# Chunk bounds and selection of a quad: 576 queries in one pass in place of 192 and 384, with new instruction lists

## The chip, the cores and the metric

One core of a Trainium2 chip runs the whole kernel; seven cores are idle. The metric is the device time of one execution in microseconds (us). Each number of runs is given with its median. Before the change three runs gave 272.13 us as median (272.02 to 273.0).

## What is computed

Two layers, one after the other, for 4 batches of 768 tokens.

The first is attention with 8 heads of 64 and a choice of key chunks. Keys are cut into 24 chunks of 32. For each query and chunk an upper bound of the score is formed from the smallest and the largest key value of each dimension:

```
k_min, k_max = min and max of k over the 32 keys of a chunk
ub  = sum over d of max(q * k_min, q * k_max)          # (query, chunk)
ub  = -1e9 where the chunk lies behind the query's own
top = the 6 chunks with the largest ub
attn = softmax of q.k/8 over the keys of these chunks, causal
x   = attn @ v
```

A query of the first 192 has at most six chunks in front of it, so for it nothing has to be chosen. The choice concerns the other 576 queries.

The second is a two-layer network on the 3072 rows of 512: `h = x @ w_in` (2048 wide), `g = h where h > 0, else exp(h) - 1`, `out = g @ w_out`.

## The kernel before, in words

**Tiling.** Two heads of a batch make a pair (16 pairs, numbered 0 to 15, four to a batch); two pairs make a quad (8 quads). The 768 queries of a pair are two halves of 384. Batch 0 (`SPLIT`) is loaded, turned and prepared half by half (`first_prep`, L637): TensorE (PE) turns K and Q by transposes (L689), ScalarE (ACT) copies them out of PSUM (L699, L721, L725), VectorE (DVE) reduces the chunks' minima and maxima (L708). Pairs of batches 1 to 3 are prepared whole (`pair_prep`): DVE transposes (L607, L625) and reduces (L611), GpSimd (POOL) casts to bf16 (L741).

**Chunk bounds and selection.** `quad_sel` (L744) handles a quad and a half: the first half has 192 queries that need a choice, the second 384. Its steps are:

- PE forms the bounds of the quad's four heads (L771, 16 matmuls in float32 of 64 rows by 32 columns, the even and odd blocks of queries on different columns of the array) into one of two double PSUM buffers, `S2`.
- DVE transposes them into `ubt` (L788), sets the query's own chunk and those behind it to a very low value (L793), takes the eight largest of each block of 32 queries (L800, 6 or 12 instructions), compares the bounds with the sixth (L805, into `selv`) and transposes the result back (L811, into `selt`).
- Four copies on POOL (L822) put the result into rows 64 to 87 of the pair's query operand (`rhs`, held by `qb`). The keys' operand holds -40000 in the matching row and chunk, so that the score matmul itself masks the keys.

**Attention.** `pair_attend` computes scores (L863, into the same two `S2` buffers), the exponential on ACT (L890), the product with V (L922), the normalisation on DVE (L935, L938), a transpose on PE (L947) and a copy on ACT (L950) into `xT`. In batch 0 the diagonal is masked by PE (L869), later by POOL (L909).

**The network.** `mlp` runs for each batch and half: 16 blocks of four up-matmuls (L972), exponential (L982) and two DVE steps each (L1011 and L1016, or L987 on ACT and L990), then 12 groups of four down-matmuls (L1032), copies (L1041) and stores (L1046). It starts when the transposed attention output of its half is complete; batch 0's network runs beside batch 1's attention, and so on.

**What sets the order.** Every step is a numbered operation of a planner (`Plan`, L156), numbered in the order of the `add` calls. `QUEUE` (L52) is a list of these numbers for each engine, written out by hand: each engine issues its operations in exactly that order. The planner's durations only decide how the engines' lists are interleaved in the program and which buffer of a class an operation takes (`caps`, L405: for instance two `S2`, two `ubt`). PE, ACT, DVE and POOL each run their list in order, and SP starts most loads and all stores; four early Q loads are started by ACT. `PAUSE`, `ALONE` and `late` describe to the planner when loads arrive.

Of the kernel before, what the change touches and what calls it, by code (L numbers as in the profile page):

```python
# [74 lines left out]
    ],  # L75
    "POOL": [
# [12 lines left out]
    ],  # L89
    "ACT": [  # L90
# [20 lines left out]
    ],  # L111
# [5 lines left out]
    ],  # L117
# [43 lines left out]
class Plan:  # L161
# [71 lines left out]
    SHARE = {128: 1.0, 256: 0.35, 512: 0.3, 768: 0.3, 1024: 0.3, 2048: 0.5}  # L233
    HEAVY = 0.088
    RAMP = 240.0
    PAUSE = ((15.8,16.6),(21.9,22.7),(29.8,30.8))
    LANDED = 0.75

    def served(self, rings, t, until):
# [154 lines left out]
def kernel(  # L394
# [349 lines left out]
    def quad_sel(g, hf):  # L744

        pairs = (2 * g, 2 * g + 1)
        if hf == 0:
            SELT[g], = new("selt")
# [366 lines left out]
```

## Time and profile before

| | |
|---|---|
| median of 3 runs | 272.13 us |
| the profiled execution | 271.44 us |
| its span | 269.6 us |
| PE busy | 260.3 us |
| DVE busy | 207.2 us |
| ACT busy | 200.6 us |
| POOL busy | 122.3 us |
| matmuls for the chunk bounds (L771), all 16 calls | 512 records |

The profiled execution lasts a little longer than the span that its trace covers. Busy times of one engine overlap at their ends, since the next instruction starts while the last one drains, so a busy engine is not always at its peak. In a row of the chain of waits or of a timeline stand the start, the length, the engine, the line and the operation; in a row by line stand the shapes, the count, the busy time in us, the mean of one in ns, and the idle time before. In the table by stage, each engine's busy time and number of instructions follow the stage's length; the last three columns are the granted clock, the share of DMA and GB/s.

### The profile page before, as it was taken

The numbers are of one execution on the slowest core, as the hardware profiler recorded it, in microseconds if no ns is written. First come the engines' busy times: TensorE is split into PE (matmuls) and PEld (weight loads), VectorE is DVE, ScalarE is ACT, GpSimd is POOL, SyncE is SP. The second block draws the span as 40 slices with busy tenths as digits, with TensorE's granted clock in tenths as the row PEclk, the third lists the DMA queues.
The fourth block names the chain that finished last, engine by engine and source line by source line (L and its number), as shares of the span: only waits on it lengthen the run. The fifth ranks groups of instructions, "written<-read, shape, count | busy, mean of one in ns | idle before, by whom it ended". The sixth has DMA issues, their size and how long they took to land.

```text
span 269.6 us, 7062 instructions
## 1 busy us (share of the span) xinstructions
PE 260.3 (97%) x2648; PEld 162.8 (60%) x2648; DVE 207.2 (77%) x562; ACT 200.6 (74%) x375; POOL 122.3 (45%) x233
## 2 busy tenths in 40 slices
PE   4998899999999999999999999999999999999995
PEld 3986566655566655655655566565666555654544
DVE  5789899899999999999898946686666785444440
ACT  4899899757996989998999386986888843234322
POOL 3697971175995798745871167434610000000000
PEclk9999999999999999999999999999999999999999
DMA  7998999989996998999621020000030100102103
GB/s 222 268 233 118 203 215 213 182 165 163 186 174 106 191 212 152 165 180 221 127 80 41 0 80 0 2 2 1 2 117 4 39 0 24 58 2 78 72 6 119
DMA packets 112626, 29.82 MB, mean 111 GB/s; under 512 B 101200, under 2 KB 109648, under 8 KB 112592
## 3 DMA queue, kind: packets, MB, share of 16 engines
q1 hardware_dynamic: 107280, 24.39, 46.0%
q0 software_dynamic: 4224, 4.19, 9.4%
q10 hardware_dynamic: 1088, 0.79, 0.9%
q8 instruction: 21, 0.34, 0.6%
q14 instruction: 13, 0.11, 0.1%
HBM read 27.26 MB, written 6.29 MB: 124 GB/s over the span
## 4 chain that ended last, share of the span: by engine, by line
PE 90%; ACT 5%; DVE 2%; DMA 1%; issue 1%; POOL 0%; ACTq 0%
PE psH L972 23%; PE psM L1032 23%; PE psS L863 13%; PE psO L922 8%; PE psS L972 8%; PE psMT L1032 8%; PE psS L771 3%; ACT lhs L699 2%; ACT pt L890 2%; PE psT L947 2%; DMA gT<-in_k_dram 1%; PE psMT L689 1%; PE psH L689 1%; PE psS L869 1%; ACT qa L725 0%
## 5 line engine op out<-in xcount | busy, mean ns | idle before, releaser
L890 ACT ACTIVATE pt<-psS 128x768 bf16<-128x768 f32 (+2 forms) x120 | 89.9, 777 | 7.7 <-PE psO L922 4.0
L972 PE MATMUL psH<-xT,w_in_sb 128*128 128x384 bf16 x384 | 75.0, 326 | 0.0
L1032 PE MATMUL psM<-w_out_sb,gT 128*128 128x512 bf16 x288 | 71.8, 379 | 0.0
L972 PEld LDWEIGHTS <-w_in_sb 128*128 128x128 bf16 x512 | 47.8, 97 | 33.0 <-issue 1.2
L1032 PEld LDWEIGHTS <-gT 128*128 128x128 bf16 x400 | 37.4, 97 | 33.6
L982 ACT ACTIVATE f<-psH 128x384 f32<-128x384 f32 x96 | 48.1, 505 | 10.8 <-PE psH L972 8.8
L863 PE MATMUL psS<-rhs,lhs 88*128 88x384 bf16 (+4 forms) x304 | 54.5, 283 | 0.7 <-ACT pt L890 0.5
L909 POOL TENSOR_SCALAR_AFFINE_SELECT pt<-pt 128x512 bf16<-128x512 bf16 (+1 forms) x48 | 24.6, 521 | 48.3 <-ACT pt L890 47.6
L1011 DVE SCALAR_TENSOR_TENSOR t<-f,psH 128x384 bf16<-128x384 f32 x56 | 30.2, 544 | 10.8 <-ACT f L982 10.0
L822 POOL COPY rhs<-selt 24x192 bf16<-24x192 bf16 (+1 forms) x64 | 27.2, 424 | 22.2 <-DVE selt L811 19.6
L863 PEld LDWEIGHTS <-lhs 88*128 88x128 bf16 x304 | 27.6, 97 | 14.6 <-ACT pt L890 1.5
L741 POOL CAST rhs<-f 64x768 bf16<-64x768 f32 (+1 forms) x40 | 28.2, 706 | 13.4 <-DVE f L625 6.5
L1016 DVE SCALAR_TENSOR_TENSOR gT<-psH,t 128x384 bf16<-128x384 f32 x56 | 30.5, 549 | 1.0
L922 PEld LDWEIGHTS <-pt 128*128 128x128 bf16 x672 | 27.2, 98 | 6.0 <-ACT pt L890 0.6
L922 PE MATMUL psO<-vext,pt 128*128 128x65 bf16 x672 | 29.7, 194 | 0.3 <-ACT pt L890 0.2
L741 POOL CAST lhs<-f 64x768 bf16<-64x768 f32 x24 | 19.7, 821 | 12.1 <-DVE f L607 11.1
L982 ACT ACTIVATE f<-psS 128x768 f32<-128x768 f32 x16 | 12.9, 811 | 16.5 <-PE psS L972 16.4
L990 DVE SCALAR_TENSOR_TENSOR gT<-f,psH 128x384 bf16<-128x384 f32 x40 | 21.6, 543 | 3.6 <-ACT psH L987 3.1
L972 PE MATMUL psS<-xT,w_in_sb 128*128 128x384 bf16 x128 | 22.9, 326 | 0.0
L1000 DVE TENSOR_SCALAR t<-f 128x768 bf16<-128x768 f32 x16 | 8.9, 558 | 17.5 <-ACT f L982 17.5
L1032 PE MATMUL psMT<-w_out_sb,gT 128*128 128x512 bf16 (+1 forms) x112 | 22.1, 349 | 0.0
L950 ACT ACTIVATE xT<-psT 128x384 bf16<-128x384 bf16 x32 | 15.4, 498 | 8.4 <-PE psT L947 8.3
(55 smaller groups left out, 299.3 us busy)
## 6 DMA issues: line engine op xcount, KB each, us to landing
out_dram<-osb SPq DMA_DIRECT2D x23, 256.0 KB, 2.3
f<-in_k_dram SPq DMA_DIRECT2D x48, 96.0 KB, 4.1
f<-in_q_dram SPq DMA_DIRECT2D x48, 96.0 KB, 3.5
f<-in_v_dram SPq DMA_DIRECT2D x24, 192.0 KB, 3.8
w_in_sb<-in_moe_w_in_dram POOLq DMA_DIRECT2D x4, 512.0 KB, 8.0
w_out_sb<-in_moe_w_out_dram POOLq DMA_DIRECT2D x4, 512.0 KB, 12.4
gT<-in_k_dram SPq DMA_DIRECT2D x8, 192.0 KB, 4.0
gT<-in_v_dram SPq DMA_DIRECT2D x12, 128.0 KB, 4.3
```

The source lines that it names most:

```text
L741: nc.gpsimd.tensor_copy(out=o, in_=i)
L822: eng.tensor_copy(out=dst.rearrange("c h (i two x) -> c h i two x", two=2, x=32)[:, :, :, odd, :], in_=tiles[st][r0:r0 + NCH, c0:c0 + n].r ...
L863: nc.tensor.matmul(p_s[:, hd, pc:pc + w], lhsT=tiles[pt_["kb"]][0:64 + NCH, hd, 128 * kb:128 * kb + 128], rhs=tiles[pt_["qb"]][0:64 + NCH, ...
L890: lambda bs=bs, pt=pt, wtot=wtot, lo=lo, at=at: nc.scalar.activation(out=tiles[pt][:, :, lo:lo + wtot], in_=tiles[bs[0]][:, :, at:at + wto ...
L909: nc.gpsimd.affine_select(out=a, in_=a, compare_op=AOT.is_ge, fill=0.0, base=0, pattern=pat, channel_multiplier=-1)
L922: nc.tensor.matmul(po[:, hd, qi, :], lhsT=tiles[pt][:, hd, off:off + 128], rhs=tiles[pt_["vx"]][:, 6 * hd + kb, :], start=(kb == 0), stop= ...
L972: nc.tensor.matmul(ph, lhsT=w_in_sb[:, kk, f0:f0 + 128], rhs=tiles[XT[4 * b + kk]][:, c0:c0 + HALF], start=(kk == 0), stop=(kk == NKK - 1))
L982: lambda e=e, view=view: nc.scalar.activation(out=halves(e)[:, 0:step], in_=view(), func=AF.Exp),
L990: lambda e=e, view=view, fc=fc, gt=gt: nc.vector.scalar_tensor_tensor(out=tiles[gt][:, fc:fc + step, :], in0=halves(e)[:, 0:step], scalar= ...
L1011: lambda e=e, t=t, view=view: nc.vector.scalar_tensor_tensor(out=tiles[t][:, 0:step], in0=halves(e)[:, 0:step], scalar=1.0, in1=view(), op ...
L1016: lambda t=t, view=view, fc=fc, gt=gt: nc.vector.scalar_tensor_tensor(out=tiles[gt][:, fc:fc + step, :], in0=view(), scalar=0.0, in1=tiles ...
L1032: nc.tensor.matmul(pm, lhsT=tiles[gt][:, fc, 128 * tt:128 * tt + 128], rhs=w_out_sb[:, fc, x0:x1], start=(fc == 0), stop=(fc == NFC - 1))
```

## The change

For batches 1 to 3, whose pairs are prepared whole, `quad_sel` is called once for a quad with `hf = None`: 576 queries in one pass. So one call of 16 matmuls of 288 columns stands for two calls of 96 and 192 columns, one transpose into `ubt` for two, 18 maxima for 6 and 12, one comparison for two, one transpose back for two, and four copies on POOL of 24 x 576 for eight. In batch 0 the two halves stay. That is nine operations fewer for each of six quads, 54 in all (6 on PE, 24 on DVE, 24 on POOL).

`ubt`, `thr` and `selv` grow to 18 blocks; `ubt` and `thr` have one buffer in place of two.

The lists of all engines are new. All numbers behind the first selection of batch 1 are shifted; apart from that the order itself differs, in batch 0 too: DVE writes the zero rows ahead of the diagonal's tile, POOL makes the diagonal second in place of third, SP loads K of pair 0's second half second, PE issues the bounds of batch 0's second quad (operation 122) two places earlier and turns K of pair 0's second half before the first scores. The planner's description of loads is changed (`ALONE`, `PAUSE`, no `late`); it emits no instruction.

```diff
 QUEUE = {
     "DVE": [
-        0, 6, 7, 9, 11, 12, 8, 10, 22, 23, 24, 38, 39, 40, 56, 57, 82, 83, 58, 72, 73, 172, 74, 173, 84, 85,
+        6, 0, 7, 8, 11, 9, 12, 10, 22, 23, 38, 39, 40, 24, 56, 57, 82, 58, 72, 73, 83, 172, 74, 84, 173, 85,
...
     "POOL": [
-        3, 5, 1, 4, 28, 29, 44, 45, 30, 62, 46, 63, 78, 64, 80, 79, 179, 178, 87, 86, 88, 89, 180, 194, 195,
+        3, 1, 5, 4, 28, 29, 30, 44, 62, 45, 46, 78, 79, 63, 64, 179, 194, 86, 87, 195, 80, 178, 129, 127, 130,
...
     "SP": [
-        13, 31, 47, 163, 65, 17, 51, 165, 183, 215, 181, 197, 167, 217, 199, 201, 511, 513, 528, 530, 545, 559,
...
+        13, 163, 31, 47, 17, 65, 165, 217, 183, 51, 181, 197, 201, 215, 199, 511, 167, 513, 528, 530, 545, 525,
...
     "PE": [
-        19, 25, 41, 35, 53, 59, 69, 90, 75, 81, 169, 106, 175, 131, 185, 191, 203, 122, 147, 93, 219, 209, 109,
...
+        19, 25, 35, 41, 59, 53, 69, 75, 169, 81, 106, 175, 90, 191, 185, 122, 203, 131, 93, 209, 219, 225, 147,
...
-            "ubt": 2, "thr": 2, "selv": 2, "selt": 2, "pt": 10, "t": 3, "gT": 3,
+            "ubt": 1, "thr": 1, "selv": 2, "selt": 2, "pt": 10, "t": 3, "gT": 3,
...
-        "selv": [const.tile([P, 12, 32], BF16, name=f"selv{i}") for i in range(caps["selv"])],
+        "selv": [const.tile([P, 18, 32], BF16, name=f"selv{i}") for i in range(caps["selv"])],
...
-        "kx": ([P, NCH], F32), "ubt": ([P, 12, 32], F32), "thr": ([P, 12, 8], F32),
+        "kx": ([P, NCH], F32), "ubt": ([P, 18, 32], F32), "thr": ([P, 18, 8], F32),
...
     def quad_sel(g, hf):
 
         pairs = (2 * g, 2 * g + 1)
+        whole = hf is None
+        hs = (0, 1) if whole else (hf,)
+        end = whole or hf == 1
+        hf = 0 if whole else hf
...
-            n = HALF - SEL0 if hf == 0 else HALF
+            n = S - SEL0 if whole else HALF - SEL0 if hf == 0 else HALF
...
             for u in pairs:
-                rd += [PAIR[u]["qt", hf], PAIR[u]["qa", hf], (PAIR[u]["km"], 0, hf), (PAIR[u]["km"], 1, hf)]
-                if hf or u in SPLIT:
-                    fr += [PAIR[u]["qt", hf], PAIR[u]["qa", hf]]
-                if hf:
+                rd += [PAIR[u]["qt", hf], PAIR[u]["qa", hf]] + [(PAIR[u]["km"], i, x) for i in range(2) for x in hs]
+                fr += [PAIR[u]["qt", hf], PAIR[u]["qa", hf]]
+                if end:
                     fr += [PAIR[u]["km"]]
...
-                        reads=[(st, hf)], writes=[(qb, hf, odd, "left")], free=[st] if hf and j and odd else [],
+                        reads=[(st, x) for x in hs], writes=[(qb, x, odd, "left") for x in hs],
+                        free=[st] if end and j and odd else [],
...
             for g in (2 * b, 2 * b + 1):
-                for hf in range(2):
-                    quad_sel(g, hf)
+                quad_sel(g, None)
                 for u in (2 * g, 2 * g + 1):
                     for hf in range(2):
                         pair_attend(u, hf)
```

More of the change, by code (lines that the diff above doesn't have):

```diff
@@ L230, in clocked @@
         return dur if warm else dur + dur
-    ALONE = {128: 0.0138, 256: 0.0194, 512: 0.036, 768: 0.038, 1024: 0.055, 2048: 0.085}
+    ALONE = {128: 0.0138, 256: 0.0188, 512: 0.036, 768: 0.0368, 1024: 0.055, 2048: 0.085}
     SHARE = {128: 1.0, 256: 0.35, 512: 0.3, 768: 0.3, 1024: 0.3, 2048: 0.5}
@@ L235 @@
     RAMP = 240.0
-    PAUSE = ((15.8,16.6),(21.9,22.7),(29.8,30.8))
+    PAUSE = ((0.0, 2.28), (17.2, 17.8), (21.6, 22.4), (30.5, 31.3))
     LANDED = 0.75
@@ L571, in weights, with fetch @@
         add("DMA", 0.0, -20.0, lambda: None, reads=[("asked", i)], writes=[name], lat=plan.LANDED)
-    def fetch(starts, packets, size, pr, f, writes, eng="SP", more=(), late=0.0, **kw):
+    def fetch(starts, packets, size, pr, f, writes, eng="SP", more=(), **kw):
         uid[0] += 1
@@ L577, in fetch @@
         add(eng, 0.533 * starts, pr, f, reads=more, writes=[w] + writes, lat=0.0,
-            move=(0 if eng == "SP" else 1, (1.08 if eng == "SP" else 1.3) + late, 0.533, starts, packets, size), **kw)
+            move=(0 if eng == "SP" else 1, 1.08 if eng == "SP" else 1.3, 0.533, starts, packets, size), **kw)
         add("DMA", 0.0, pr, lambda: None, reads=[w], writes=writes, lat=plan.LANDED)
@@ L674, in first_prep @@
         early = u - SPLIT[0] < EARLY[hf]
-        late = 0.35 if u == SPLIT[0] and hf == 0 else 0.0
-        fetch(1, 256, 768, pl, load(i0, kr), [(sg, i0)], late=late, alloc=[sg] if u == SPLIT[0] else [])
+        fetch(1, 256, 768, pl, load(i0, kr), [(sg, i0)], alloc=[sg] if u == SPLIT[0] else [])
         fetch(1, 256, 768, (pl + 0.1) - 300.0 * early, load(i0 + 1, qr, nc.scalar if early else nc.sync), [(sg, i0 + 1)],
-              eng="ACT" if early else "SP", late=late)
+              eng="ACT" if early else "SP")
         if u % 2 == 0:
@@ L776, in quad_sel @@
             for u in pairs:
-                rd += [PAIR[u]["qt", hf], PAIR[u]["qa", hf], (PAIR[u]["km"], 0, hf), (PAIR[u]["km"], 1, hf)]
-                if hf or u in SPLIT:
-                    fr += [PAIR[u]["qt", hf], PAIR[u]["qa", hf]]
-                if hf:
+                rd += [PAIR[u]["qt", hf], PAIR[u]["qa", hf]] + [(PAIR[u]["km"], i, x) for i in range(2) for x in hs]
+                fr += [PAIR[u]["qt", hf], PAIR[u]["qa", hf]]
+                if end:
                     fr += [PAIR[u]["km"]]
-            add("PE", 0.0025 * n + 0.073, pr, ub, reads=rd, writes=[bu[0]], alloc=bu, free=fr)
+            add("PE", 0.00167 * n + 0.27, pr, ub, reads=rd, writes=[bu[0]], alloc=bu, free=fr)
             ut, = new("ubt")
@@ L812, in t2 @@
                                     in_=tiles[sv].rearrange("p a b -> p (a b)")[:, 0:n])
-            add("DVE", dve(n), pr, t2, reads=[sv], writes=[(st, hf)], alloc=[] if hf else [st], free=[sv])
+            add("DVE", dve(n), pr, t2, reads=[sv], writes=[(st, x) for x in hs], alloc=[] if hf else [st], free=[sv])
             for j, u in enumerate(pairs):
```

165 rows, old and new, of the table QUEUE are left out of this document.

## The prediction

> **What bounds the kernel now.** I read the page first: its head, the busy times, the forty slices.
>
> ```profile
> span 269.6 us, 7062 instructions
> PE 260.3 (97%) x2648; PEld 162.8 (60%) x2648; DVE 207.2 (77%) x562; ACT 200.6 (74%) x375; POOL 122.3 (45%) x233
> PE   4998899999999999999999999999999999999995
> PEclk9999999999999999999999999999999999999999
> ```
>
> TensorE is busy 97% of the span at full granted clock. To see whether it is dense where the change acts, I cut the span into stages (us, then busy time of PE, PEld, DVE, ACT, POOL):
>
> ```profile
> 10.00:20.00 10.00, 9.67 (x163) 8.77 (x160) 8.27 (x36) 9.82 (x26) 7.94 (x18) 1.00 1.14 250
> 20.00:32.50 12.50, 10.80 (x189) 7.88 (x187) 11.67 (x51) 11.56 (x24) 10.44 (x20) 1.00 1.03 156
> 32.50:60.00 27.50, 27.50 (x336) 17.95 (x334) 25.40 (x56) 23.49 (x44) 12.64 (x20) 1.00 1.22 193
> 60.00:100.00 40.00, 39.99 (x432) 23.73 (x416) 39.79 (x107) 33.68 (x61) 30.77 (x56) 1.00 1.01 173
> 100.00:140.00 40.00, 40.00 (x434) 24.11 (x411) 37.75 (x109) 37.28 (x75) 29.35 (x51) 1.00 0.87 161
> 140.00:266.40 126.40, 126.34 (x1108) 74.72 (x1105) 78.35 (x188) 78.84 (x140) 26.74 (x52) 1.00 0.09 33
> ```
>
> From 32.5 to 266.4 us PE has no idle time. So two things set the end: when this dense stretch begins, and how much PE work lies in it. But from 60 to 100 us DVE too is full, 39.79 of 40. The chain of waits and the timelines show how close that is (start, length, what):
>
> ```profile
> 4.04 1.51 PE psH L689 x6
> 5.55 2.56 PE psMT L689 x12
> 8.11 0.82 PE psH L689 x6
> ...
> 32.49 1.30 PE psH L972 x8
> ...
> 255.94 10.41 PE psMT L1032 x64
> ```
> ```profile
> 94.85 1.02 DVE L938 TENSOR_TENSOR on<-psO,rc 128x384 bf16<-128x384 f32 x2
> ```
> ```profile
> 95.87 0.33 PE L947 MATMUL psT<-ident_b,on 128*128 128x128 bf16 x3
> ```
>
> DVE ends a normalisation at 95.87 and PE transposes it at 95.87: no slack. Any DVE work put ahead of that point stalls PE unless DVE idles less earlier.
>
> **What the change takes from PE.** It merges two chunk-bound calls (L771) of each of six quads, batches 1 to 3, into one. Their price, from the chain:
>
> ```profile
> 58.02 0.49 PE psS L771 x32
> 58.51 0.97 PE psM L1032 x4
> 59.48 0.81 PE psS L771 x32
> 60.29 1.41 PE psH L972 x8
> 61.70 1.73 PE psM L1032 x8
> ...
> 79.89 1.28 PE psS L771 x64
> ...
> 144.75 1.32 PE psS L771 x64
> 146.07 1.41 PE psH L972 x8
> ```
>
> A call with 192 queries takes 0.49, one with 384 takes 0.81. And what follows a call is 0.11 longer than usual: four L1032 matmuls 0.97 where eight take 1.73 (0.86 for four), eight L972 1.41 where eight take 1.30. The line through both sizes is 0.17 + 0.00167 per query, so 576 queries take 1.13, with the 0.11 behind it 1.24. Four quads have their calls apart: 0.49 + 0.11 + 0.81 + 0.11 = 1.52, each saves 0.28. Two (at 79.89 and 144.75) have them back to back: 1.30 + 0.11 = 1.41, each saves 0.17. Sum 4 x 0.28 + 2 x 0.17 = **1.46 us**. No call of 576 is in the trace. If the small call is held up by something that doesn't scale down, and time goes with queries from 384 on, it takes 0.81 x 1.5 = 1.22, and the sum is 4 x 0.19 + 2 x 0.08 = 0.9. I take the line, since both known sizes lie on it by construction and nothing shows a floor; 0.9 stays an end of the range. As PE has no gap behind, a microsecond less of PE work is a microsecond.
>
> **What it takes from DVE and POOL.** The means by shape:
>
> ```profile
> L822 POOL COPY rhs<-selt 24x384 bf16<-24x384 bf16 x32 | 16.0, 501 | 2.9 <-DVE selt L811 1.6
> L822 POOL COPY rhs<-selt 24x192 bf16<-24x192 bf16 x32 | 11.1, 348 | 19.3 <-DVE selt L811 18.0
> L788 DVE STREAM_TRANSPOSE ubt<-psS 128x384 f32<-128x384 f32 x8 | 4.6, 572 | 0.0
> L811 DVE STREAM_TRANSPOSE selt<-selv 128x384 bf16<-128x384 bf16 x8 | 4.5, 564 | 0.1
> L805 DVE TENSOR_TENSOR selv<-ubt,thr 128x288 bf16<-128x288 f32 x8 | 3.6, 454 | 0.1
> L788 DVE STREAM_TRANSPOSE ubt<-psS 128x192 f32<-128x192 f32 x8 | 3.0, 375 | 3.9 <-PE psS L771 3.9
> L811 DVE STREAM_TRANSPOSE selt<-selv 128x192 bf16<-128x192 bf16 x8 | 2.9, 362 | 0.1
> L805 DVE TENSOR_TENSOR selv<-ubt,thr 128x144 bf16<-128x144 f32 x8 | 2.5, 309 | 0.1
> L793 DVE MEMSET ubt<- 64x6 f32 x16 | 0.6, 63 | 0.1
> ```
>
> By the same lines one instruction of 576 takes 0.77 (L788) for 0.95, 0.77 (L811) for 0.93, 0.60 (L805) for 0.76; two memsets of 0.06 go. The 18 maxima stay. That is 0.62 per quad by busy times; neighbours on DVE overlap by some 0.08, so 0.35 is the lower end. For six quads 2.1 to 3.7 us of DVE, on no path of the end by itself, but it loosens the full stage. POOL makes four copies of 0.65 for eight (2.6 for 3.4): 0.8 per quad. POOL is 77% busy from 60 to 100, so I cost that at nothing.
>
> Buffers: `ubt` and `thr` have one in place of two. Writer and readers of both are DVE instructions in one order, so it costs nothing unless two selections interleave; the new DVE list has none that do. The merged call holds one of two S2 slots of PSUM for 1.13 + 0.77 in place of twice for less; the sum is smaller.
>
> **Start.** Two `selv` memsets on POOL grow from 0.42 to about 0.63, and the diagonal is made behind them and behind DVE's zero rows: ready near 2.6 us. The first transpose waits for its load until 4.04, which hides it. On SP the second K load is now that of pair 0's second half, pair 1's is third, and pair 3's comes behind three V loads.
>
> ```profile
> 1.81 0.97 SPq L666 DMA_DIRECT2D gT<-in_k_dram  x2
> ```
> ```profile
> 4.21 0.37 SPq L666 DMA_DIRECT2D gT<-in_k_dram  x1
> ```
> ```profile
> DMA to landing us min/median/max: 3.1/4.3/5.3
> ```
>
> The third load was issued at 1.81 and lands near 6.1; PE wants pair 1's K at 4.04 + 1.51 + 1.28 = 6.83. Pair 3's moves from 4.21 to about 5.7 and lands near 10.0, when PE wants it (it turned that pair at about 10.1): between 0 and 0.9 late. ACT, which carries the chain behind it (9.82 of 10), has other turns to copy, so I take 0. The work listed ahead of the first MLP matmul is the same set on PE and on ACT; only its order differs. PE's idle time between 4.04 and 32.5 is 2 us in all, so the order can gain at most about 2 and, from the loads, lose about 1. I take 0.
>
> **Sum.** 269.6 - 1.5 = 268.1 of span; around the span lie 271.44 - 269.6 = 1.84: 270.0 against the profiled 271.44. The median of the runs, 272.13, is 0.69 above that execution, so the median should be **270.6** (0.5% is 1.36 us, about what a measurement can tell from no change: faster means below 270.77).
>
> **Rivals.**
>
> 1. DVE becomes the bound and eats it. I compared which instructions stand ahead of the normalisation of pair 7's first half in both DVE lists. The new one has two more reductions and one more transpose of 768 columns (0.9 each), one normalisation less (0.5), and two quads' savings (0.7 to 1.2): 0.5 to 1.5 more, while PE has about 0.3 less ahead. With no slack at that place that is a stall of up to 1.5, and the time about **272.0**. Against it: DVE idles 1.73 + 0.83 + 2.10 = 4.7 us from 10 to 60, and the new lists put batch 0's second bounds call two places earlier on PE, for which DVE waited 0.9. If DVE idles 1.3 less, nothing stalls. Chance 0.22.
>
> 2. The merged selection is late (slower). The first scores of a pair now wait for all 576 queries. Before: 0.49 for the call, then on DVE 0.38, 0.07, six maxima, 0.31, 0.36 and a copy of 0.35, some 2.5. After: 1.13 + 0.77 + 0.13 + 18 x 0.088 + 0.60 + 0.77 + 0.65 = 5.6.
>
> ```profile
> 23.62 1.05 DVE thr L800 x12
> ```
>
>    (1.05 for twelve gives 0.088.) By the new PE list the work between the call's start and the first scores that need it, added up from the chain's pieces (0.65 for four L972, 0.86 for four L1032, 0.03 for one L922, 0.16 for a score matmul of 384), is 8.0, 7.3, 9.9, 17.6, 20 and 13 us for the six quads, and one or two MLP instructions of 0.5 stand between on DVE in the first two. So the margins are about 2, 1 and 3; it decides when DVE comes to the transpose over 1 to 2 us behind the call. PE's list is fixed, so it then stands. One microsecond in each of four quads up to 115 us gives 270.6 + 4 = **274.6**. For it: DVE full from 60 to 100. Against: at 58.6 DVE waited for the call, not the call's result for DVE. Chance 0.17.
>
> 3. The new order of batch 0 gains half of PE's 2 us: **269.6**. Chance 0.12.
>
> 4. Longer holds of a shared port. L805 reads two SBUF tensors, and L715, which does too, shows spread.
>
> ```profile
> L715 DVE TENSOR_TENSOR km<-kx,km 128x12 f32<-128x12 f32 x8 | 2.3, 297 | 0.1
> ```
>
>    0.30 for twelve columns is far above what they need, while POOL copies; so a DVE instruction of this kind seems to wait for a running POOL copy, now up to 0.65. Once per quad in four quads of the full stage is 2.6: 270.6 + 2.6 = **273.2**. Against: copies and such instructions become fewer, and L805's means (0.31, 0.45) lie on a line with its size, which leaves little waiting. Chance 0.04. The Trainium skill, SBUF — State Buffer, the section with the practical consequences of the port rules, says that a Vector instruction with two SBUF inputs contends with a GpSimd instruction that reads SBUF, and that the loser blocks for the whole instruction; L715's row agrees, L805's shows hardly any of it.
>
> That the change doesn't do what it says is the 0.9 us sum above: 271.2, within the forecast.
>
> **Chances and range.** Forecast (PE dense throughout, 270.0 to 271.2): 0.45; rivals 0.22, 0.17, 0.12, 0.04. Faster by over 0.5%: 0.12 and three quarters of 0.45, 0.46. Within 0.5%: the rest of it, rivals 1 and 4, 0.37. Slower: 0.17. The range takes in rivals 1 and 3 and the smaller delays of 2: 269.2 to 273.4.
>
> **What would show it.** Right: L771 in batches 1 to 3 at about 1.13 per call, six calls, PE without gaps from about 32.4 on, DVE some 2 us less busy, POOL some 4. Rival 1: idle time of PE before L947 or L1032, released by DVE, from 75 to 115. Rival 2: PE idle before L863 released by POOL's L822. Rival 3: the first L972 before 31.5. Rival 4: L805 above 0.7. Wrong in size if a call takes 1.2 or if the 0.11 behind it grows.

## The result and the profile after

After the change 22 runs gave a median of 273.3 us (272.63 to 274.9), 22 runs of the kernel before on the same chip 272.09 (270.95 to 273.18). The ratio is 1.0044, 95% interval 1.0029 to 1.006: about 1.2 us slower, where 1.5 us less was forecast. Ratios here and below are formed from runs in the chip's faster state; one of the twelve runs of experiments 4 and 13 was in the slower one. The profiled execution took 273.46 us with a span of 271.8, against 271.44 and 269.6 before.

Head, busy times and granted clock of the page of the kernel after:

```profile
span 271.8 us, 6603 instructions
PE 258.6 (95%) x2456; PEld 160.0 (59%) x2456; DVE 206.8 (76%) x532; ACT 200.0 (74%) x375; POOL 118.3 (44%) x209
PEclk9999999999999999999999999999999999999999
```

PE is busy 1.7 us less than before, POOL 4.0, and DVE only 0.4; the granted clock is full. PE's busy time went down about as the prediction had it, and the span went up by 2.2 us all the same. So PE idles more. The table by stage shows where (the first row is of the kernel before, whose later stages stand in the prediction; the others are of the kernel after):

```profile
0.00:10.00 10.00, 5.96 (x36) 5.58 (x37) 5.97 (x22) 5.53 (x11) 4.42 (x21) 1.00 0.91 233
```
```profile
0.00:10.00 10.00, 5.68 (x36) 5.00 (x36) 6.39 (x22) 5.48 (x11) 3.58 (x19) 1.00 0.89 234
10.00:20.00 10.00, 8.94 (x151) 7.92 (x149) 7.56 (x35) 9.00 (x24) 7.60 (x16) 1.00 1.16 237
20.00:32.50 12.50, 10.57 (x195) 8.35 (x193) 11.38 (x43) 11.87 (x26) 10.89 (x21) 1.00 1.02 155
32.50:60.00 27.50, 27.01 (x306) 17.41 (x304) 24.70 (x57) 22.96 (x44) 12.22 (x21) 1.00 1.23 196
60.00:100.00 40.00, 38.00 (x341) 21.90 (x339) 38.08 (x103) 30.72 (x54) 28.86 (x45) 1.00 1.15 160
100.00:140.00 40.00, 40.00 (x382) 23.80 (x381) 37.84 (x99) 37.15 (x75) 25.57 (x41) 1.00 0.91 175
```

Up to 32.5 us PE idles 7.3 us where it idled 6.1 (+1.2); from 32.5 to 60, 0.5 where it was nothing; from 60 to 100, 2.0 where it was 0.01; behind that nothing. The sum is +3.7, less 1.7 of busy time saved: 2.0 of the 2.2.

Not all of that 1.7 is the merge's. The 96 transposes of batch 0 (L689, after the change L685), which the merge doesn't touch, make up 0.9 of it: in the rows by line they take 26.4 us before and 25.5 after, and 27.6 in experiment 1, whose list for PE is that of the kernel after. A sounder measure starts at the first merged call. What PE has to do from there on is the same before and after, but for the merge and for four down-matmuls (0.86 us) that the old order has already done by then. PE is busy 208.38 us from there before (from 57.95), 207.96 after (from 58.48) and 207.70 in experiment 1 (from 58.95). So the merge takes 1.3 to 1.5 us from PE. By the same reckoning the kernel after comes to that call 1.4 us late (58.48 for 57.95 less 0.86), loses 2.0 from 60 to 100 and gains 1.3: 2.1 of the 2.2.

PE's waits behind 30 us by what released them (sum, times, longest) name the last two stages:

```profile
PE psS L863 <- ACT pt L890: 1.8, 3, 1.4
PE psT L947 <- DVE on L938: 0.8, 1, 0.8
PE psH L972 <- DMA w_in_sb<-in_moe_w_in_dram: 0.4, 1, 0.4
```

The wait of 1.4 us for an exponential is no slow exponential. The chain of waits of the kernel after, over that stretch (start, length, what), and SP's timeline:

```profile
86.95 0.53 DVE gT L990
...
89.19 0.59 SPq L592
...
89.82 3.55 DMA out_dram<-osb
...
93.39 0.60 ACT osb L1041
93.99 1.41 ACT pt L890 x2
...
95.44 0.48 PE psS L863 x2
```
```profile
84.84 4.94 SPq L592 DMA_DIRECT2D f<-in_k_dram  x8
89.82 0.61 SPq L1046 DMA_DIRECT2D out_dram<-osb  x1
```

Read it backwards. PE waits for ACT; ACT stands with a copy into `osb` at the head of its list, and two exponentials behind it; the copy waits 1.74 us for a store to land, because `osb` has three buffers; the store is issued at 89.82, since SP's list has eight K loads in front of it and issues them one after the other, from 84.84 to 89.78. Waiting for a free buffer `f` has little part in that: the waits that the profile names there are 0.7 us in all, and four loads took as much time each before the change (2.53, below). ACT's and PE's rows:

```profile
93.39 0.60 ACT L1041 ACTIVATE osb<-psM 128x512 f32<-128x512 f32 x1 [1.74 <-DMA out_dram<-osb]
```
```profile
94.74 0.49 PE L863 MATMUL psS<-rhs,lhs 88*128 88x384 bf16 x2 [1.36 <-ACT pt L890]
```

Before, SP issued the first such store at 86.75, ahead of its loads, and the copy didn't wait:

```profile
86.75 0.53 SPq L1046 DMA_DIRECT2D out_dram<-osb  x1
87.38 2.53 SPq L595 DMA_DIRECT2D f<-in_q_dram  x4
```

At the start, pair 3's K is the eighth transfer on SP, and PE stands when it comes to it. SP's and PE's rows after:

```profile
0.81 1.97 SPq L663 DMA_DIRECT2D gT<-in_k_dram  x4
4.43 1.56 SPq L668 DMA_DIRECT2D gT<-in_v_dram  x3
6.04 0.51 SPq L663 DMA_DIRECT2D gT<-in_k_dram  x1
```
```profile
11.13 0.85 PE L685 MATMUL psH<-ident_f,gT 128*128 128x128 f32 x6 [0.87 <-ACT qa L721]
```

The row names ACT, whose copy ends at 11.01. Pair 3's K, issued at 6.04, was under way for 5.0 us and landed at 11.0 as well, so this trace doesn't tell the two apart. The first bounds call starts at 13.21 against 12.03 before. And the first up-matmuls wait for the second part of `w_in`, issued at 27.32 (chain of waits):

```profile
27.32 8.23 DMA w_in_sb<-in_moe_w_in_dram
```

Before, that part was issued no earlier, at 27.54, but landed after 6.9 us.

### The profile page after: what moved, and what is told of

The parts are those of the page before. It is cut to its first block, busy times and chain, and to the rows that moved or that the text cites. A ratio compares the mean times of both kernels' runs of the same rounds, so it can differ in the third digit from the quotient of the medians.

```text
span 271.8 us, 6603 instructions
## 1 busy us (share of the span) xinstructions
PE 258.6 (95%) x2456; PEld 160.0 (59%) x2456; DVE 206.8 (76%) x532; ACT 200.0 (74%) x375; POOL 118.3 (44%) x209
## 4 chain that ended last, share of the span: by engine, by line
PE 78%; ACT 7%; DVE 6%; DMA 6%; issue 1%; SPq 1%; POOL 0%; DVEq 0%; ACTq 0%; POOLq 0%
PE psH L972 20%; PE psM L1032 20%; PE psS L863 10%; PE psS L972 8%; PE psMT L1032 8%; PE psO L922 6%; ACT pt L890 3%; DMA w_in_sb<-in_moe_w_in_dram 3%; PE psS L771 2%; ACT lhs L695 2%; PE psT L947 2%; DMA out_dram<-osb 1%; PE psMT L685 1%; DMA gT<-in_k_dram 1%; PE psH L685 1%
## 5 line engine op out<-in xcount | busy, mean ns | idle before, releaser
L890 ACT ACTIVATE pt<-psS 128x768 bf16<-128x768 f32 (+1 forms) x120 | 89.8, 781 | 11.3 <-PE psS L863 6.7
L972 PE MATMUL psH<-xT,w_in_sb 128*128 128x384 bf16 x384 | 73.7, 326 | 0.5 <-DMA w_in_sb<-in_moe_w_in_dram 0.4
L982 ACT ACTIVATE f<-psH 128x384 f32<-128x384 f32 x96 | 47.0, 506 | 7.0 <-PE psH L972 6.1
L821 POOL COPY rhs<-selt 24x576 bf16<-24x576 bf16 (+2 forms) x40 | 22.7, 566 | 24.2 <-DVE selt L810 22.5
L922 PEld LDWEIGHTS <-pt 128*128 128x128 bf16 x672 | 28.3, 98 | 7.4 <-issue 1.0
L1016 DVE SCALAR_TENSOR_TENSOR gT<-psH,t 128x384 bf16<-128x384 f32 x56 | 30.5, 551 | 1.1
L922 PE MATMUL psO<-vext,pt 128*128 128x65 bf16 x672 | 31.1, 194 | 0.1
L987 ACT ACTIVATE psH<-psH 128x384 f32<-128x384 f32 x40 | 20.2, 512 | 0.0
```

Source lines behind the costliest of these rows:

```text
L821: eng.tensor_copy(out=dst.rearrange("c h (i two x) -> c h i two x", two=2, x=32)[:, :, :, odd, :], in_=tiles[st][r0:r0 + NCH, c0:c0 + n].r ...
L890: lambda bs=bs, pt=pt, wtot=wtot, lo=lo, at=at: nc.scalar.activation(out=tiles[pt][:, :, lo:lo + wtot], in_=tiles[bs[0]][:, :, at:at + wto ...
L922: nc.tensor.matmul(po[:, hd, qi, :], lhsT=tiles[pt][:, hd, off:off + 128], rhs=tiles[pt_["vx"]][:, 6 * hd + kb, :], start=(kb == 0), stop= ...
L972: nc.tensor.matmul(ph, lhsT=w_in_sb[:, kk, f0:f0 + 128], rhs=tiles[XT[4 * b + kk]][:, c0:c0 + HALF], start=(kk == 0), stop=(kk == NKK - 1))
L982: lambda e=e, view=view: nc.scalar.activation(out=halves(e)[:, 0:step], in_=view(), func=AF.Exp),
L1016: lambda t=t, view=view, fc=fc, gt=gt: nc.vector.scalar_tensor_tensor(out=tiles[gt][:, fc:fc + step, :], in0=view(), scalar=0.0, in1=tiles ...
```

## Experiments

Each kernel is the changed one with one edit, unless said otherwise; ratios are to the kernel before, run on the same chip (272.0 to 272.44 us as median); they are not quotients of the medians and differ from these by up to 0.003. Where lists are shown, they are pieces of `QUEUE` in the new numbering. The merge in the old lists wasn't tried: the old order has two selections open at once, and with 18 blocks there is only one `ubt`.

**1. The store ahead of the loads.** Operation 428 is the store, 947 and 964 are two load operations of four transfers each.

```diff
 "SP"
-        932, 947, 964, 428, 927
+        932, 428, 947, 964, 927
```

> The changed kernel with one edit: on SP the store of batch 0's third row block (operation 428 by the old numbers) is issued ahead of the K loads of pairs 10 and 11, in place of behind them. Theory S (the store stands behind loads that wait for a free f buffer, the osb ring of three is then full, ACT waits 1.7 us for the store and PE 1.6 us for ACT's exponentials): ACT's wait for out_dram near 92 us is gone, PE's idle time from 60 to 100 us falls from 2.0 to about 0.4, and the time falls by 1.3 to 2.0 us, to 271.3 to 272.0, level with the kernel before. Theory M (the merged selection itself is late, so PE waits for DVE and POOL whatever the store does): the wait for the store goes, but PE idles as long in front of L863 or L947, and the time stays within 0.4 us of 273.3.

Measured: 272.49 us (12 runs), ratio 1.0000 (0.9976 to 1.0023). From 1.0044 that is 1.2 us, by the profiled spans (271.8 and 270.4) 1.4, by the two medians 0.8; the two intervals lie apart. SP's timeline and the stage of this kernel:

```profile
84.84 0.48 SPq L1042 DMA_DIRECT2D out_dram<-osb  x1
85.42 4.91 SPq L588 DMA_DIRECT2D f<-in_k_dram  x8
```
```profile
60.00:100.00 40.00, 39.57 (x361) 22.86 (x354) 39.66 (x105) 31.78 (x56) 30.25 (x48) 1.00 1.07 159
```

One store moved past two load operations (eight transfers) brings PE from 38.00 to 39.57 of 40. The late store is shown as the largest single cause. What is left is that the kernel is now only level with the one before, though PE has some 1.5 us less to do.

**2 and 3. The old order of batch 0.** All operations of batch 0 up to the weights' loads stand in the old order in the places that they have in the new lists, on all engines; the third kernel has the early store too.

```diff
 "SP", "PE", "ACT", "DVE", "POOL"
-        (operations up to 330 in the new order)
+        (the same places, the operations in the old order)
```

> The changed kernel, but batch 0's loads, preparation, selection and attention (all operations numbered up to 330) stand in the order of the kernel before, on all engines, in the places that these operations have in the new lists. Theory D (the new order of batch 0 costs 1 us at the start, because pair 3's K load comes behind three V loads and its turn waits for a PSUM bank): the first bounds call moves from 13.2 to about 12.1 us, PE is busy 0.7 us more between 10 and 20, and the time falls by 0.8 to 1.1 us, to 272.2 to 272.5. Rival (the start doesn't matter because DVE is the bound from 60 to 100 us): the early microsecond is lost again before 100 us and the time falls by less than 0.3.

> Both edits together: the old order of batch 0 and the store ahead of the loads. If the two causes are separate and PE's work is 1.5 us less than before, the time falls by 2.2 to 3.0 us from 273.3, to 270.3 to 271.1, that is 0.995 of the kernel before. If one stall hides the other, it falls by no more than 1.8.

Measured: 277.32 us (6 runs), ratio 1.0181 (1.0144 to 1.0219), and 277.7, ratio 1.0195 (1.0155 to 1.0236). A miss: the first bounds call did come earlier (12.54, for 13.21 after the change), and the time rose by 4 us. PE is busy 23.68 us from 32.5 to 60 in place of 27.01. Its longest wait there, in the first of the two:

```profile
PE psS L859 <- ACT pt L886: 3.4, 4, 1.0
```

So the new batch 0 isn't simply worse: an old piece doesn't fit between the new ones, and where lists of five engines interlock, exchanging one stretch in all of them says little of that stretch. From here on one or two operations are moved at a time.

**4. Only SP's loads of batch 0 in the old order.**

```diff
 "SP"
-        13, 163, 31, 47, 17, 65, 165, 217, 183, 51, 181, 197, 201, 215, 199, 511, 167,
+        13, 31, 47, 163, 65, 17, 51, 165, 183, 215, 181, 197, 167, 217, 199, 511, 201,
```

> The changed kernel, with only SP's loads of batch 0 in the old order; PE, ACT, DVE and POOL keep the new lists. If the start is late because of the loads (pair 3's K), the first bounds call comes at about 12.3 us and the time falls by 0.6 to 1.0. If it is late because of the order on PE and ACT (a PSUM bank that ACT gives back late), the first bounds call stays at about 13.2 and the time stays within 0.3 of 273.3.

Measured: 272.93 us (12 runs), ratio 1.0023 (0.9997 to 1.005). In its profile PE comes to the first bounds call without a stall, 0.76 earlier than after the change (13.21):

```profile
11.70 0.82 PE L681 MATMUL psH<-ident_f,gT 128*128 128x128 f32 x6
12.45 0.40 PE L767 MATMUL psS<-f,km 64*32 64x96 f32 x16
```

The ratio's interval overlaps that of the changed kernel, so a gain in time is not shown.

**5. Both edits of SP's list** (1 and 4).

> The changed kernel with two edits in SP's list alone: batch 0's loads in the old order, and the store ahead of the K loads of pairs 10 and 11. Adding up over the start of six bounds calls, the old loads gained 0.75 us and the early store 1.4. If the two causes are separate, PE's lost time against the kernel before falls from 3.8 to about 1.5, which is what the merge takes from PE, and the time is 271.2 to 272.0, 0.997 to 1.000 of the kernel before. If DVE is the bound from 60 to 100 us, the earlier start is lost there and the time is that of the early store alone, 272.3 or more.

Measured: 272.54 us (12 runs), ratio 1.0011 (0.9982 to 1.0041): no gain over the first. PE's longest wait from 30 to 60 us:

```profile
PE psH L972 <- DMA w_in_sb<-in_moe_w_in_dram: 1.2, 1, 1.2
```

In this profile the first bounds call comes at 12.98, and the second part of `w_in`, issued at 27.10, lands after 9.1 us. So what was gained at the start is spent on waiting for the weights, 1.2 us in place of 0.4.

**6. Weights earlier, ahead of batch 0's last casts.** The fifth kernel, and on POOL both first parts of `w_in` (331, 333) moved up, the first from 24.6 to 21.6 us.

```diff
 "POOL"
-        128, 212, 213, 229, 331, 228, 238, 237, 333, 335
+        128, 331, 212, 213, 229, 333, 228, 238, 237, 335
```

> As the one before, and on POOL the first two quarters of w_in are asked for earlier: the first ahead of the casts of pair 2's second half, the second ahead of a cast of pair 3's second half. Theory W (the first MLP matmuls wait for w_in): PE's wait for the weights near 35 us (0.4 to 0.7) goes, the bounds call of quad 2 comes 0.4 to 0.6 earlier, and the time falls by as much against the kernel with the two SP edits. Rival: the 1.5 us that the two DMA starts take on POOL delay batch 0's casts and copies, and the time stays or rises by up to 1.

Measured: 272.39 us (12 runs), ratio 1.0017 (0.999 to 1.0044). The wait for `w_in` is gone; ahead of 32.5 us PE now waits for a Q load:

```profile
PE psMT L685 <- DMA gT<-in_q_dram: 0.9, 1, 0.9
```

That the earlier weights delay the Q load is not shown by this: PE waits for a Q load in runs 7, 10 and 12 too (1.7, 1.1 and 0.9 us), whose weights stand at their old place.

**7. The merge undone in four quads.** The fifth kernel, with quads 2, 3, 4 and 7 in two calls, the second one's operations right behind the first one's in each list. (The buffers of a split quad are freed at its second call, as before the change.)

```diff
-                quad_sel(g, None)
+                for hf in (None,) if g in (5, 6) else (0, 1):
+                    quad_sel(g, hf)
```

> The kernel with the two SP edits, but quads 2, 3, 4 and 7 run their bounds and selection in two calls of 192 and 384, back to back, as before the change (the second half's steps right behind the first's on DVE and POOL); quads 5 and 6 stay merged. It tells what the merge by itself is worth. Theory F (the merge takes PE work away and costs nothing): 0.17 us of PE per quad come back, 0.7 in all, and with the DVE work of three quads in the full stage (0.35 to 0.62 each) up to 1.9 more: 0.7 to 2.5 slower than the kernel with the two SP edits. Theory M (the merged selection delays the first scores, and that is the loss): it is faster, by 0.5 or more.

Measured: 279.58 us (5 runs), ratio 1.0249 (1.0208 to 1.029), some 7 us more than the fifth, several times the price of the calls. So undoing the merge in these lists makes the kernel slower, not faster, against theory M; but 7 us for four quads is no price of engine time either. Runs 9 to 11 take it apart.

**8. One MLP step ahead of quad 3's selection on DVE.** The sixth kernel with operation 480 (L1016) ahead of the merged transpose 665, behind which PE's weight load stood 0.6 us.

```diff
 "DVE"
-        479, 665, 480, 666
+        479, 480, 665, 666
```

> As the kernel with earlier weights, and on DVE the second step of an MLP block (operation 480) ahead of quad 3's merged transpose in place of behind it. PE stood 0.25 us at that place, waiting for the PSUM bank which that step frees behind the transpose of 0.77. If this is the cost of the longer DVE instructions, PE's gap near 83 us goes and the time falls by 0.2 to 0.3, which the runs can hardly tell, but the trace can: no idle PE between 80 and 90 us.

Measured: 272.38 us (12 runs), ratio 1.0024 (0.9996 to 1.0051): the same as the sixth. No gain.

**9, 10, 11. One quad in two calls at a time,** in the first kernel (early store): quad 3, quad 4, quad 7.

```diff
-                quad_sel(g, None)
+                for hf in (0, 1) if g == 3 else (None,):
+                    quad_sel(g, hf)
```

> The lists with the early store (272.5), but quad 3 alone runs in two calls of 192 and 384 one behind the other, with its two sets of DVE steps and eight POOL copies. Theory PE (only TensorE's time counts, as the prediction had it): +0.17 us for the second call, 272.6 to 272.8. Theory DVE (around 80 us DVE is as full as TensorE, and the selection's longer DVE work of 0.62 us, with the wait for its result, shows in the end): +0.5 to +1.8, 273.0 to 274.3, with idle time of PE between 80 and 105 us that ends at DVE, ACT or POOL.

> As before, but quad 4 alone (bounds at about 101 us) runs in two calls. Theory PE: +0.17 us, 272.6 to 272.8. Theory DVE: +0.5 to +1.8, 273.0 to 274.3, with idle time of PE between 100 and 120 us.

> As before, but quad 7 alone (bounds at about 178 us) runs in two calls. Behind 140 us DVE has time to spare and no MLP work of batch 1 waits, so theory PE and theory DVE both give +0.17 to +0.4 us, 272.6 to 272.9; more than +0.6 speaks against both and for a buffer that the second call holds longer.

Measured: 272.41 us (12 runs), ratio 1.0021 (1.0002 to 1.004); 274.78 (6 runs), 1.0096 (1.0073 to 1.0119); 276.26 (6 runs), 1.0154 (1.0126 to 1.0182). Against the first kernel's 272.49: -0.1, +2.3, +3.8 (by the ratios +0.6, +2.6, +4.2). Quad 3 bears out a small price of the call and can't tell 0.17 from nothing. Quad 4 lies above theory DVE's range but shows its sign, PE idling for DVE and ACT. PE's waits in its profile:

```profile
PE psH L973 <- DVE gT L991: 0.8, 1, 0.8
PE psH L973 <- ACT osb L1042: 0.7, 1, 0.7
PE psT L948 <- DVE gT L991: 0.3, 1, 0.3
PE psH L973 <- DVE gT L1017: 0.3, 1, 0.3
```

They lie between 109 and 119 us, and none is for an exponential. On DVE the second set of selection steps runs from 106.8 to 109.7, and the MLP steps for which PE waits stand behind it. Quad 7 lies far above both theories. PE's timeline there, behind its two calls at 178.34 and 179.69:

```profile
178.34 0.40 PE L771 MATMUL psS<-f,km 64*32 64x96 f32 x16
...
179.69 0.56 PE L771 MATMUL psS<-f,km 64*32 64x192 f32 x16 [0.79 <-ACT pt L891]
...
183.21 0.48 PE L864 MATMUL psS<-rhs,lhs 88*128 88x384 bf16 x2 [0.90 <-ACT pt L891]
...
186.50 0.48 PE L864 MATMUL psS<-rhs,lhs 88*128 88x384 bf16 x2 [0.96 <-ACT pt L891]
...
190.65 0.33 PE L948 MATMUL psT<-ident_b,on 128*128 128x128 bf16 x3 [0.58 <-DVE gT L991]
```

Together 3.2 of the 3.8 us, 2.65 of it for exponentials. A second call takes a second turn of the two `S2` buffers. It has to wait until the exponential has emptied the other one. Then its bounds stay there until DVE has transposed them, from 187.10 to 187.64, since on DVE the second set stands behind the first; for these 8 us all score tiles go through the one other buffer, and two of them wait for the exponential that empties it. The last wait is again for an MLP step behind the second set on DVE. In quad 4 the second call's bounds stayed 6 us (101.01 to 107.36), and no score tile waited. So these runs don't price the engines' work: they show what a second set of steps costs in lists that were written for one, in two ways and in two of three places.

**12. A known price on PE.** The first kernel with each merged call's 16 matmuls issued twice, with the same values.

```diff
-                for w in range(2):
+                for w in (0, 1, 0, 1) if n > HALF else (0, 1):
```

> The lists with the early store, and each of the six merged bounds calls issues its 16 matmuls twice into the same PSUM tile (the same values), so 6 x 0.96 = 5.8 us of TensorE time are added and nothing else. Theory PE (TensorE is dense from 32.5 us on, so its time counts in full): 277.8 to 278.8. Theory slack (TensorE waits in the full stage for DVE's and ACT's results, so that part of its time is hidden): under 276.5, with less idle time of PE than in the kernel with the early store.

Measured: 278.09 us (4 runs), ratio 1.0207 (1.0182 to 1.0232): 5.6 us more than the first kernel, for 5.8 of added work (a doubled call takes 2.10 us, 0.97 more). Its stages:

```profile
60.00:100.00 40.00, 39.57 (x417) 22.93 (x402) 37.75 (x101) 29.90 (x53) 28.51 (x44) 1.00 1.08 162
...
140.00:260.00 120.00, 120.00 (x1061) 70.72 (x1060) 79.63 (x181) 81.33 (x146) 30.73 (x52) 1.00 0.07 25
```

PE's time counts in full in this region. So the 1.5 us that the merge saves there should count as well, and what eats them lies, but for the 0.4 us of idle time between 60 and 100, ahead of 60 us: by the reckoning above, run 1 comes to its first merged call at 58.95, 1.9 us late.

**13, 14, 15. The second part of `w_in` alone earlier,** right behind the first, which keeps its place: in the fifth kernel, in the first, and in the first with the eighth's edit of DVE.

```diff
 "POOL"
-        331, 228, 238, 237, 333, 335
+        331, 333, 228, 238, 237, 335
```

> Both edits of SP's list (store early, loads of batch 0 in the old order), and on POOL the load of the second part of w_in directly behind the first, so about 1.6 us earlier (25.5 in place of 27.1 us), behind the loads of batch 0 and not ahead of them. Theory order (what is left of the loss ahead of 59 us is the place of that one load: TensorE stood 1.2 us for it): the wait goes, no wait for Q loads comes, 271.3 to 271.8. Theory bandwidth (the loads ahead of 35 us share what the transfers can carry, and an earlier weight load only moves the wait to another load): 272.2 to 272.7, with some 0.7 to 1.5 us of idle time of PE elsewhere ahead of 59 us.

> The store early, the loads of batch 0 in the new order, and the second part of w_in directly behind the first on POOL. Theory order: the wait of 0.7 us goes, 271.6 to 272.0. Theory bandwidth: 272.2 to 272.7.

> As the kernel just before, and on DVE one MLP step (the product for gT) ahead of quad 3's merged transpose, behind which PE and ACT wait near 83 us. Theory order: 0.2 us less than the kernel just before. Theory bandwidth: the same as it, since PE's idle time near 83 us is only some 0.2 us already.

Measured, 12 runs each, against 272.44: 271.79 us, ratio 0.9975 (0.9952 to 0.9998); 271.74, 0.9984 (0.9968 to 1.0000); 271.7, 0.9989 (0.9967 to 1.0011). All three are below the kernel before, the first by an interval that leaves 1 out, and all are 0.5 to 0.7% below the changed kernel's 1.0044. The wait for `w_in` is gone in each; in run 13's profile a wait of 1.3 us for a Q load stands in its place, which theory order had excluded, in run 14's one of 0.3. PE's waits from 32.5 to 60 us in the second:

```profile
PE psS L863 <- ACT pt L890: 0.4, 1, 0.4
```

From 1.0000 to 0.9984 is 0.4 us, from 1.0011 to 0.9975 1.0; the intervals overlap, so that this one move helps is likely and not certain. The edit on DVE adds nothing. The start still isn't that of before: in the second kernel the first bounds call comes at 13.20 and the first merged call at 58.44, 1.4 us late.

## Why the prediction was wrong

**The part on the merge held.** A call of 576 queries was to take 1.13; the chain of waits of the kernel after has

```profile
58.55 1.13 PE psS L771 x32
...
147.09 1.13 PE psS L771 x32
```

and from the first merged call on PE has 1.3 to 1.5 us less to do, for 1.46 forecast. That its busy time over the whole span fell by 1.7 is close by luck, as 0.9 of it lies in the transposes of batch 0. On DVE and POOL, by line and shape:

```profile
L787 DVE STREAM_TRANSPOSE ubt<-psS 128x576 f32<-128x576 f32 x6 | 4.7, 779 | 0.2
L810 DVE STREAM_TRANSPOSE selt<-selv 128x576 bf16<-128x576 bf16 x6 | 4.6, 773 | 0.1
L804 DVE TENSOR_TENSOR selv<-ubt,thr 128x432 bf16<-128x432 f32 x6 | 4.3, 712 | 0.1
L821 POOL COPY rhs<-selt 24x576 bf16<-24x576 bf16 x24 | 15.9, 662 | 21.0 <-DVE selt L810 20.1
```

0.78, 0.77 and 0.66 for 0.77, 0.77 and 0.65. Only the comparison is off, 0.71 for 0.60, through one instance. Added up over the rows by line and shape, DVE's work fell by 4.0 us (235.8 to 231.8), 2.3 of it in the selection's transposes and memsets, within the 2.1 to 3.7 forecast; the engine's busy time, which counts overlapping neighbours once, fell only by 0.4.

**The step that failed** is the one that turns work into time: "As PE has no gap behind, a microsecond less of PE work is a microsecond." That PE had no gap was read from a trace of the old lists. The change made all lists anew, SP's among them, and the prediction looked into SP's list only for the loads of the first 10 us. The stores weren't looked at, nor the three `osb` buffers through which a late store reaches ACT. In the fixed lists the sentence is right (run 12: 5.6 of 5.8 us); for the new ones it lacked +2.0 us of idle time from 60 to 100, of which one store moved past two load operations gives back 1.6 (run 1), and the 1.4 us by which it comes late to the first merged call.

**"Start. ... I take 0"** failed as well in the profile, within the bounds that it gave itself: pair 3's K was bounded at 0 to 0.9 late. It was issued at 6.04 for 5.7 and under way for 5.0 us for 4.3, so it landed at 11.0, and PE, which would have taken it at 10.26, stands 0.87 there. The old load order brings the first call 0.76 earlier (run 4). But an earlier start by itself isn't worth its size: in run 5 it was spent on waiting for the weights, whose loads on POOL the prediction didn't follow either. With the weights moved, what is left of the forecast's 1.5 us is 0.3 to 0.7.

**Rivals.** The first (DVE eats it) is not borne out: from 75 to 115 PE waits for DVE only 0.25 us, near 83, behind quad 3's merged transpose; its 0.8 us for a normalisation lie near 31 us, where the kernel before had 0.9 in two pieces. The second (the merged selection late) is not borne out: no wait of PE behind 30 us is released by POOL's copies. Its time, slower than before, came for another reason. The third (the new batch 0 gains) went the other way in the profile. The fourth, the shared port, shows once among the six merged calls, behind 140 us where DVE has time to spare. DVE's and POOL's timelines:

```profile
157.06 1.28 DVE L804 TENSOR_TENSOR selv<-ubt,thr 128x432 bf16<-128x432 f32 x1
```
```profile
157.06 0.82 POOL L737 CAST lhs<-f 64x768 bf16<-64x768 f32 x1
```

Both start at 157.06, and the comparison takes 1.28 where the other five take 0.60, 0.68 more, which is most of the cast's 0.82. The Trainium skill, SBUF — State Buffer, section "SBUF: two separate sides", says that the pair of ports is an exclusive lock, that whichever starts first holds it for the whole instruction, and that the other fully blocks; this pair of rows agrees.

**What stays open.** The start. The first bounds call came at 12.69 to 14.34 us in five profiles with one and the same start of the lists (runs 1 and 9 to 12), and the wait for a Q load in them is between 0 and 1.1 us. With SP's old order of loads it came earlier, at 11.91 to 12.98 (runs 4 to 8 and 13). But that is not kept: the first call of quad 2, behind the same list of PE, starts at 57.84 to 59.58 in those six profiles, and at 58.26 to 59.55 in the eight with the new order of loads. Also, the one profile of the kernel before is of an execution 0.65 us below its median. So how much of the loss ahead of 60 us belongs to the new order of which list, and how much to when loads happened to land, these runs don't settle.

## What to carry to other kernels

When a change replaces hand-written lists, a "dense" engine of the old trace is no premise for the new kernel: go through every list that can hold up a buffer, the one that only issues transfers among them. In each, look for an instruction whose buffer someone waits for (here a store) behind a run of others that take their time to issue (here eight loads, 4.9 us), and follow the ring of buffers to the engine at its end. Undoing a merge inside lists that were written for it prices those lists, not the merge. And compare work from a point that both kernels reach with the same work done: the busy time of untouched instructions can differ by more than the change.

## What the runs showed of the hardware

- Issuing a transfer takes time on SP: eight loads in front of a store took 4.94 us, 0.47 to 0.82 each. The store went out at 89.82 in place of 84.84, and cost PE, three steps away, 1.6 us of idle time.
- A bounds call of 16 float32 matmuls keeps to the line of 0.17 us and 0.00167 us per query up to 576 queries (1.13 us in each of five calls of the chain).
- The 96 float32 transposes of batch 0 take 25.5, 27.6 and 25.2 us of PE's time in three profiles with one and the same list of PE (after, runs 1 and 12), at a granted clock of 1.00. The reason is open.
- The second part of `w_in` landed 6.9 to 9.1 us after its issue in four profiles (before, after, runs 1 and 5). Issued 1.7 us earlier (run 14) it was not waited for.
- Splitting one bounds call in two, with the second set of steps right behind the first, cost 2.3 and 3.8 us in two places and no more than 0.6 in a third. In the costliest, the second call's bounds stood in one of two PSUM buffers for 8 us, and PE waited 2.65 us for exponentials.
